# One DMA queue in a listed order, and batch 1's affine pass on ScalarE, in the backward pass of a strided convolution with group norm and GELU

## The chip, the cores and the metric

The kernel runs on 1 core of one Trainium2 chip. The metric is the device time of one execution in microseconds, from the launch's first to its last instruction. The core has a matrix engine (TensorE, PE in the profile; its weight loads are PEld), three engines for elementwise work (VectorE or DVE, ScalarE or ACT, GpSimd or POOL), and SyncE (SP), which here issues transfers only. Each engine runs its own instructions in the order in which they were emitted and waits on semaphores for the others.

## The reference

Forward and backward of a convolution stem: two sequences of 16,000 positions and 256 channels, a kernel of 31 taps with stride 2, a normalisation of each channel over the positions, and GELU.

```python
L = (T - K) // s + 1                       # 7985 positions out, K = 31, s = 2
h = einsum('blc,cd->bld', x[:, 0:s*L:s], w[0])
for i in range(1, K):
    h = h + einsum('blc,cd->bld', x[:, i:i + s*L:s], w[i])
mu  = h.sum(1) / L
var = ((h - mu) ** 2).sum(1) / L
h = (h - mu) / sqrt(var + 1e-5) * gn_gamma + gn_beta
out = gelu(h)                              # tanh form
```

The kernel returns `out` and, for a given `grad_out`, the gradients of `x`, `w`, `gn_gamma` and `gn_beta` (`out_0` to `out_4`). All data is bf16.

## The kernel before, in words

The work runs in five stages, whose names the planner uses. **F0** and **F1** are the forward convolution of batch 0 and batch 1, **G0** and **G1** the gradient of x for the two batches, and **W** is the gradient of w. Each batch's sequence is cut into four chunks of 2,048 output positions. The convolutions are done with fewer multiplications, by a scheme of sums and differences in three nested levels: each level has three branches, called A, B and C, and B uses a sum of the two others' inputs. VectorE forms the sums (`f_sums` L472, `g_sums` L985, `w_add` L1251, `pair_x`, `pair_d` and the subtractions L1413), TensorE multiplies (`f_mm` L508, `g_mm` L1033, `w_mm` L1289), and VectorE combines the branches in PSUM (`ve` L583 and `ve_neg` L587, called by `f_seed` and `g_seed`). ScalarE moves finished banks out of PSUM (`keep` L591, `f_evac` L611 and L624, and the copies L540, L573, L1060, L1070, L1370). PSUM has four slots of two banks, `ring`, which are taken in turn.

- *x.* `x_load` (L399) brings a chunk of x transposed into the one buffer `XT` by `turn` (L344), a transposing transfer on SP: one transfer of 2.2 MB for a chunk, but four of a quarter's size for the very first.
- *h.* The forward stores h in the DRAM tiles `hd` and its sums for the statistics (`fwd_stats`).
- *GELU.* `gelu_batch` (L790) goes through a batch in 16 units (`gelu_unit` L829). A unit loads h (L833, on ACT's own queue), works with five ScalarE instructions (L836, L838, L842, L844, L860) and some ten of VectorE (L840, L846, L850, L862), stores the gradient of h's normalised form in `dyd`, and the output in out_0 (batch 0, turned on SP) or in `yd` (batch 1, turned later by `out0_late`). Batch 0's units run beside F1, batch 1's beside G0.
- *Gradient with respect to h.* `e_load` (L928) brings a chunk of `dyd` and `hd` (1 MB each), `e_comp` (L932) forms dy*a + h*b + c by two affine passes (L938, L941) and an addition (L943), and `spread` (L950) copies the result into `ET`, the layout that TensorE reads: four copies a chunk, on ACT for batch 0 (L953) and on VectorE for batch 1 (L955), by `COPY`. `dn_turn` (L977) turns the same chunk and stores it in `dnd`.
- *Second differences.* `d2_piece` (L1180) loads a piece of `dnd`, forms differences of it (L1196) and stores them in `d2d` by five transfers; there are seven pieces for a batch, with one buffer `DT` for the piece and one or two for the differences. W reads `d2d` in two loads a step (`d_tile`) and x in 1 MB loads (`x_raw`). Seven pieces of batch 0 and seven of batch 1 run beside G1.

The order of all this is not the order of the calls. `Plan.add` (L151) records each instruction with an estimated duration and the bytes that it reads and writes. `Plan.order` (L180) gives each a due time, counted back from the instructions that need its result, and then walks through the instructions as a list scheduler: at each step the engine that is free first takes, of the instructions whose inputs are ready, the one that is due first. `slack`, `look` (how many TensorE groups it may take out of turn), `pads` (how much of its spare time a transfer is held back) and `lead`, a table of shifts for kinds of instructions by stage, name and caller, set the order. `emit` (L258) gives out the instructions in the order that was found, so that each engine's queue has exactly this order. The planner's picture of the transfers is one server that takes them one after another (`server`, L237 to L240), with eight places for SP and eight for POOL.

Transfers go through three queues: plain loads and all turns through SP (hardware descriptors, q1 in the profile), stores through POOL (L341 with "POOL"; software descriptors, q0), and the loads of h in `gelu_unit` through ACT (q10). `PACE` spreads the GELU units' due times over their stage. `GO` (L1117) names the branches of the input gradient in which a second group of products is split by `g_outer`.

Of the kernel before, what the change touches and what calls it, by code (L numbers as in the profile page):

```python
# [13 lines left out]
ALU = mybir.AluOpType  # L14
# [24 lines left out]
class Plan:  # L39
# [3 lines left out]
    def __init__(self, tc):  # L43
        self.tc = tc
        self.ops = []
        self.lastw = {}
        self.readers = {}
        self.pe = 0.0
        self.slack = 120.0
        self.hold = -1  # L50
        self.look = 11
        self.pads = (270.0, 253.5, 0.0)
        self.lead = {
            "F0 f_mm f_leaf": 4.0,
            "F0 f_mm f_outer": -1.5,
            "F0 f_mm f_three_ac": 5.5,
            "F0 f_mm pe_turn": 7.5,
            "F0 f_three_b forward": -7.5,
            "F0 keep f_evac": -4.0,
            "F0 load f_evac": 10.5,  # L60
            "F0 load load_w": -2.5,
            "F0 load put": 2.0,
            "F0 tt f_sums": 7.5,
            "F0 tt third": -5.0,
            "F0 turn w2_part": -1.5,
            "F0 turn x_load": -5.0,
            "F0 ve f_seed": -2.0,
            "F0 w_sub f_first": 7.5,
            "F1 f_evac last": -7.5,
            "F1 f_mm f_leaf": -5.0,  # L70
            "F1 f_mm f_three_ac": 1.5,
            "F1 gelu_unit gelu_batch": -3.0,
            "F1 load gelu_unit": 2.5,
            "F1 tiny fwd_stats": -4.0,
            "F1 tt gelu_unit": 1.0,
            "F1 turn gelu_batch": -6.5,
            "F1 turn x_load": -5.0,
            "F1 ve f_seed": 6.5,
            "F1 zero gelu_batch": 11.0,
            "G0 e_comp conv_stem_kernel": -3.0,  # L80
            "G0 g_mm g_leaf": -11.0,
            "G0 g_mm g_three_ac": 5.0,
            "G0 g_mm g_three_b": -4.0,
            "G0 gelu_unit gelu_batch": -0.5,
            "G0 keep g_evac": -3.5,
            "G0 load dgb_store": 7.0,
            "G0 load dn_turn": -8.0,
            "G0 load e_load": 4.5,
            "G0 load g_evac": -8.0,
            "G0 load gelu_unit": 10.0,  # L90
            "G0 load load_w2": 5.0,
            "G0 tiny elem_finalize": 1.5,
            "G0 tt first": 5.0,
            "G0 tt second": 6.0,
            "G0 tt third": 5.5,
            "G0 turn dgb_store": -3.0,
            "G0 turn dn_turn": 1.0,
            "G0 turn gelu_batch": -8.5,
            "G0 ve g_seed": 3.5,
            "G0 ve_neg g_seed": 8.0,  # L100
            "G1 e_comp conv_stem_kernel": -10.0,
            "G1 g_mm g_outer": 3.5,
            "G1 g_mm g_three_ac": 0.5,
            "G1 g_mm g_three_b": 0.5,
            "G1 g_three_b input_grad": 2.5,
            "G1 keep g_evac": -3.5,
            "G1 load dn_turn": 0.5,
            "G1 load e_load": -4.0,
            "G1 load g_evac": 5.5,
            "G1 spread e_comp": -9.5,  # L110
            "G1 tt first": 10.5,
            "G1 tt second": -4.5,
            "G1 tt third": -5.0,
            "G1 zero e_comp": -5.0,
            "W keep weight_grad": 4.0,
            "W load d_tile": -15.5,
            "W load w_emit": -8.5,
            "W ve w_done": 5.0,
            "W ve weight_grad": 9.0,
            "W w_add weight_grad": 2.5,  # L120
            "W w_emit w_done": 7.5,
            "W w_mm w_pairs": -1.5,
            "W w_mm w_single": -1.0,
        }
        self.overlap = {"DVE": 0.084, "ACT": 0.1}
        self.npe = 0
        self.stage = "F0"
# [23 lines left out]
    def add(self, eng, dur, outs, ins, fn, dma=None, slack=None):  # L151
# [24 lines left out]
        self.ops.append(dict(eng=eng, kind=kind, dur=dur, fn=fn, preds=preds, dma=dma, at=self.pe, hold=-1 if eng == "PE" else self.hold,  # L176
# [3 lines left out]
    def order(self):  # L180
# [7 lines left out]
        for i in range(n - 1, -1, -1):  # L188
            o = ops[i]
            full = o["dur"] + (1.3 * o["dma"] + 6.0 if o["dma"] is not None else 0.15)  # L190
            end = o["at"] if o["eng"] == "PE" else o["at"] + o["slack"]
            for s in succ[i]:
                end = min(end, due[s])
            due[i] = end - full - self.lead.get(o["kind"], 0.0)
        left = [len(o["preds"]) for o in ops]
        ready = [0.0] * n
        wait = {e: [] for e in ("PE", "DVE", "ACT", "POOL", "SP")}
        pes = [i for i, o in enumerate(ops) if o["eng"] == "PE"]
        rank = {i: k for k, i in enumerate(pes)}
        nextpe = 0  # L200
        gone = set()
        lanes = [[0.0] * 8, [0.0] * 8]
        for i in range(n):
            if not left[i]:
                wait[ops[i]["eng"]].append(i)
        free = {e: 0.0 for e in wait}
        server = 0.0
        start = [0.0] * n
        ends = [0.0] * n
        done = 0  # L210
        while done < n:
            best = None
            for e, w in wait.items():
                if e == "PE":
                    w = [i for i in w if rank[i] < nextpe + self.look]
                else:
                    w = [i for i in w if ops[i]["hold"] <= nextpe]
                if w:
                    t = max(free[e], min(ready[i] for i in w))
                    if best is None or t < best[0]:  # L220
                        best = (t, e, w)
            t, e, w = best
            i = min((i for i in w if ready[i] <= t + 1e-9), key=lambda i: (due[i], i))
            wait[e].remove(i)
            o = ops[i]
            if o["dma"] is not None:
                lane = lanes[e == "POOL"]
                t = max(t, lane.pop(0))
            start[i] = t
            end = t + o["dur"]  # L230
            free[e] = end - self.overlap.get(e, 0.0)
# [5 lines left out]
            if o["dma"] is not None:  # L237
                server = max(server, end + 1.3) + o["dma"]
                end = server + 0.9
                lane.append(end)  # L240
            ends[i] = end
            done += 1
            slip = free["PE"] - due[pes[nextpe]] - ops[pes[nextpe]]["dur"] if nextpe < len(pes) else 0.0
            for s in succ[i]:
                r = end + 0.034 * (e != "PE") if ops[s]["eng"] == e and o["dma"] is None else end + 0.12
                room = max(0.0, due[s] + slip - r)
                if ops[s]["dma"] is not None:
                    r += min(self.pads[0 if o["dma"] is None else 1], 0.3 * room)
                elif o["dma"] is not None and ops[s]["eng"] != "PE":
                    r += min(self.pads[2], 0.3 * room)  # L250
                ready[s] = max(ready[s], r)
                left[s] -= 1
                if not left[s]:
                    wait[ops[s]["eng"]].append(s)
        self.start, self.ends = start, ends
        return sorted(range(n), key=lambda i: (start[i], i))
# [13 lines left out]
def conv_stem_kernel(  # L270
# [64 lines left out]
    def dcost(nbytes, run):  # L335
        ns = {256: 18, 512: 27, 1024: 46, 2048: 85, 4096: 165}[run]
        return nbytes / run * ns / 16e3 * 1.1

    def load(out, in_, nbytes, run, eng="SP", slack=None, issue=None):
        e = {"SP": nc.sync, "POOL": nc.gpsimd, "ACT": nc.scalar}[eng]  # L340
        add(eng, issue or {"POOL": 0.8, "SP": 0.4, "ACT": 0.15}[eng], [out], [in_], lambda: e.dma_start(out=out, in_=in_),  # L341
            dma=dcost(nbytes, run), slack=slack)

    def turn(out, in_, nbytes, slack=None):  # L344
        add("SP", 1.25 + max(0, nbytes - 262144) * 6e-6, [out], [in_],
            lambda: nc.sync.dma_start_transpose(out=out, in_=in_), dma=dcost(nbytes, 256), slack=slack)
# [52 lines left out]
    def x_load(b, c):  # L399
# [4 lines left out]
        if b == 0 and c == 0:  # L404
            rows = [sb(REG + 4096 * g, 4, 512) for g in range(3)]
            for g, nm in enumerate((P, P, 16)):
                load(rows[g][0:nm], src[P * g:P * g + nm].rearrange("m (j o f) -> m j o f", j=4, o=2)[:, :, 1, :], nm * 4096, 1024)
# [5 lines left out]
        else:  # L413
            turn(flat[:, :, 0:nr], src, nr * 8192)
# [28 lines left out]
    def load_w(sl):  # L443
# [3 lines left out]
        for ch in range(2):  # L447
            for br, r1 in ((A, 0), (C_, 1)):
                i0 = 4 * r2 + 2 * r1
                for par in range(2):  # L450
# [3 lines left out]
                         65536 * nq, 512, issue=0.8)  # L454
# [471 lines left out]
    COPY = ("ACT", "DVE")  # L926
# [5 lines left out]
    def e_comp(b, c):  # L932
        et = ET[(4 * b + c) % 2]
        for dh in range(2):
            hv, ev = (t[:, dh].rearrange("p e k f -> p (e k f)") for t in (EH, EG))
            s4, s5, s6 = st(b, 4, dh), st(b, 5, dh), st(b, 6, dh)
            add("DVE", dve(2048, 4), [hv], [hv, s5, s6],
                lambda hv=hv, s5=s5, s6=s6: nc.vector.tensor_scalar(out=hv, in0=hv, scalar1=s5, scalar2=s6,  # L938
                                                                    op0=ALU.mult, op1=ALU.add))
            add("DVE", dve(2048, 4), [ev], [ev, s4],  # L940
                lambda ev=ev, s4=s4: nc.vector.tensor_scalar(out=ev, in0=ev, scalar1=s4, scalar2=None, op0=ALU.mult))  # L941
# [175 lines left out]
    GO = {(1, br) for br in (B_, C_, A, )}  # L1117
# [361 lines left out]
    PACE = ((5.0, 19.0), (391.0, 67.0))  # L1479
# [91 lines left out]
```

## Time and profile before

| what | value |
|---|---|
| time, median of 3 runs | 1235.54 us (1235.24 to 1240.54) |
| profiled execution | 1234.47 us, its span 1232.3 us |
| mean granted clock of TensorE | 0.992 |
| matmuls (PE), count and busy time | 7,846, 1195.2 us |
| DVE / ACT / POOL busy | 1010.3 / 535.8 / 203.7 us |
| moved by DMA | 263.56 MB, 214 GB/s on average |
| stages F0, F1, G0, G1, W begin at about | 0, 215, 447, 677, 890 us |
| SP transfers landing: turns of x, median | 13.6 us |
| SP transfers landing: 1 MB of x in W, median | 9.6 us |
| ACT's loads of h (256 KB), median to landing | 4.6 us |

The page has one row for each engine with its busy time. A slice row shows forty equal parts of the span, each with a digit for the busy tenths. A chain of waits follows the work that ended last back in time: 31% of the span are matmuls of the forward (L508), 27% of the weight gradient (L1289), 21% of the input gradient (L1033), and no other line has more than 2%. Two more lines from the list of waits (engine, its line, what it waited for, then the total, the number of times and the longest):

```profile
SPq L346 <- DVE arena L476: 116.6, 10, 41.8
SPq L341 <- PE ps L1289: 114.9, 25, 21.6
...
POOL out_dram L341 <- DVE arena L1321: 292.0, 14, 158.8
POOL d2d L341 <- DVE arena L1196: 110.7, 48, 8.4
```

SP and POOL spend much of their time waiting for the data of the next transfer or for its buffer.

### The profile page before, as it was taken

The numbers are of one execution on the slowest core, as the hardware profiler recorded it, in microseconds if no ns is written. First come the engines' busy times: TensorE is split into PE (matmuls) and PEld (weight loads), VectorE is DVE, ScalarE is ACT, GpSimd is POOL, SyncE is SP. The second block draws the span as 40 slices with busy tenths as digits, with TensorE's granted clock in tenths as the row PEclk, the third lists the DMA queues.
The fourth block names the chain that finished last, engine by engine and source line by source line (L and its number), as shares of the span: only waits on it lengthen the run. The fifth ranks groups of instructions, "written<-read, shape, count | busy, mean of one in ns | idle before, by whom it ended". The sixth has DMA issues, their size and how long they took to land.

```text
span 1232.3 us, 19408 instructions
## 1 busy us (share of the span) xinstructions
PE 1195.2 (97%) x7846; PEld 768.7 (62%) x7846; DVE 1010.3 (82%) x1297; ACT 535.8 (43%) x769; POOL 203.7 (17%) x321
## 2 busy tenths in 40 slices
PE   6999999899999999999999999999999999999998
PEld 4888899577676964444444444444466554566865
DVE  7988798597979859989887889888776986778883
ACT  1243344565768468888783334444322111012200
POOL 1020231011111203211210323333210000011031
PEclk8999999899999999999999999999999999999999
DMA  9642979866695896686636888886899499986562
GB/s 205 108 111 63 191 198 177 168 139 158 127 201 159 258 317 208 231 248 168 213 120 182 254 273 313 245 308 251 300 305 326 145 318 319 320 293 218 179 170 69
DMA packets 283545, 263.56 MB, mean 214 GB/s; under 512 B 186815, under 2 KB 254446, under 8 KB 275184
## 3 DMA queue, kind: packets, MB, share of 16 engines
q1 hardware_dynamic: 255808, 166.38, 52.5%
q0 software_dynamic: 23040, 87.55, 20.1%
q10 hardware_dynamic: 4608, 8.39, 2.3%
q8 instruction: 61, 1.00, 0.3%
q14 instruction: 28, 0.23, 0.1%
HBM read 129.44 MB, written 87.52 MB: 176 GB/s over the span
## 4 chain that ended last, share of the span: by engine, by line
PE 79%; DVE 6%; DMA 6%; issue 4%; ACT 2%; POOL 2%; SPq 0%; POOLq 0%; ACTq 0%; DVEq 0%
PE ps L508 31%; PE ps L1289 27%; PE ps L1033 21%; DMA d2d<-arena 2%; DMA arena<-hd 1%; DVE arena L1196 1%; POOL d2d L341 1%; DVE arena L476 1%; DMA out_dram<-arena 1%; DVE ps L583 1%; DMA arena<-in_x_dram 1%; DVE arena L466 1%; DMA arena<-arena 1%; DMA arena<-in_w_dram 1%; DVE arena L943 0%
## 5 line engine op out<-in xcount | busy, mean ns | idle before, releaser
L1033 PE MATMUL ps<-arena 128*128 128x512 bf16 (+1 forms) x2016 | 435.9, 378 | 11.8 <-DVE ps L583 8.3
L508 PE MATMUL ps<-arena 128*128 128x256 bf16 (+4 forms) x3552 | 426.7, 282 | 12.6 <-DMA arena<-in_x_dram 6.9
L508 PEld LDWEIGHTS <-arena 128*128 128x128 bf16 x3552 | 347.8, 99 | 94.4 <-issue 13.7
L1033 PEld LDWEIGHTS <-arena 128*128 128x128 bf16 x2016 | 198.0, 98 | 249.4 <-issue 20.1
L1289 PE MATMUL ps<-arena 128*128 128x256 bf16 (+1 forms) x2176 | 332.5, 313 | 0.0
L1289 PEld LDWEIGHTS <-arena 128*128 128x128 bf16 x2176 | 212.8, 98 | 112.6
L591 ACT ACTIVATE arena<-ps 128x1024 f32<-128x1024 f32 (+1 forms) x143 | 146.1, 1022 | 277.8 <-PE ps L1033 79.9
L476 DVE TENSOR_TENSOR arena<-arena 128x1087 bf16<-128x1087 bf16 (+3 forms) x194 | 163.7, 889 | 27.5 <-PE ps L508 27.2
L850 DVE TENSOR_TENSOR arena<-arena 128x1024 bf16<-128x1024 bf16 x160 | 109.0, 689 | 14.8 <-ACT arena L842 8.2
L1252 DVE TENSOR_TENSOR arena<-arena 128x4096 bf16<-128x4096 bf16 x42 | 95.8, 2288 | 25.2 <-PE ps L1289 19.6
L583 DVE TENSOR_TENSOR ps<-ps,arena 128x1024 f32<-128x1024 f32 x77 | 94.0, 1229 | 27.0 <-PE ps L1289 13.3
L341 POOL DMA_DIRECT2D out_dram<-arena x75 | 54.1, 741 | 365.7 <-DVE arena L1321 292.0
L992 DVE TENSOR_TENSOR arena<-arena 128x516 bf16<-128x516 bf16 (+3 forms) x176 | 83.5, 513 | 16.4 <-PE ps L1033 10.0
L1196 DVE TENSOR_TENSOR arena<-arena 128x768 bf16<-128x768 bf16 (+3 forms) x112 | 65.5, 642 | 16.7 <-DMA d2d<-arena 15.6
L341 POOL DMA_DIRECT2D d2d<-arena x70 | 51.0, 729 | 112.3 <-DVE arena L1196 110.7
L611 ACT ACTIVATE arena<-ps 128x512 bf16<-128x512 f32 (+1 forms) x64 | 36.8, 578 | 74.5 <-PE ps L508 74.5
L840 DVE SCALAR_TENSOR_TENSOR arena<-arena 128x1024 bf16<-128x1024 bf16 x32 | 39.2, 1224 | 20.1 <-ACT arena L838 19.8
L583 DVE TENSOR_TENSOR ps<-arena,ps 128x1024 f32<-128x1024 f32 x43 | 52.8, 1227 | 3.2 <-PE ps L1033 2.7
L1370 ACT COPY ps<-ps 128x512 f32<-128x512 f32 x28 | 16.0, 571 | 87.6 <-PE ps L1289 87.6
L1060 ACT ACTIVATE ps<-ps 128x512 f32<-128x512 f32 x48 | 27.9, 582 | 58.8 <-PE ps L1033 58.6
L1413 DVE TENSOR_TENSOR arena<-arena 128x2304 bf16<-128x2304 bf16 x36 | 48.0, 1354 | 5.5 <-PE ps L1289 5.5
L341 POOL DMA_DIRECT2D dyd<-arena x32 | 17.6, 550 | 194.2 <-DVE arena L850 189.5
(87 smaller groups left out, 785.8 us busy)
## 6 DMA issues: line engine op xcount, KB each, us to landing
arena<-in_x_dram SPq DMA_DIRECT2D x52, 1024.0 KB, 9.6
arena<-d2d SPq DMA_DIRECT2D x16, 1216.0 KB, 11.9
out_dram<-arena POOLq DMA_DIRECT2D x14, 1024.0 KB, 5.9
d2d<-arena POOLq DMA_DIRECT2D x30, 384.0 KB, 6.3
arena<-dnd SPq DMA_DIRECT2D x10, 960.0 KB, 6.4
vl<-arena POOLq DMA_DIRECT2D x36, 256.0 KB, 4.8
arena<-vl SPq DMA_DIRECT2D x9, 1024.0 KB, 8.6
hd<-arena POOLq DMA_DIRECT2D x8, 1024.0 KB, 6.3
```

What stands on the lines that cost most here:

```text
L341: add(eng, issue or {"POOL": 0.8, "SP": 0.4, "ACT": 0.15}[eng], [out], [in_], lambda: e.dma_start(out=out, in_=in_), dma=dcost(nbytes, run ...
L476: lambda: nc.vector.tensor_tensor(out=o, in0=a, in1=b, op=ALU.add))
L508: yield nc.tensor.matmul(ps[:, dh, cs], lhsT=wt, rhs=mv, start=s0, stop=False, skip_group_check=True)
L583: add("DVE", dve(1024, 1), [out], [a, b], lambda: nc.vector.tensor_tensor(out=out, in0=a, in1=b, op=op))
L591: lambda: nc.scalar.activation(out=out, in_=ps, func=ACT.Copy, scale=scale))
L850: add("DVE", dve(1024), [o], [a, b_], lambda: V.tensor_tensor(out=o, in0=a, in1=b_, op=op))
L992: lambda: nc.vector.tensor_tensor(out=o, in0=a, in1=b, op=ALU.add))
L1033: yield nc.tensor.matmul(ps[:, e, 0:wide], lhsT=lt, rhs=mv, start=s0, stop=False, skip_group_check=True)
L1196: lambda: nc.vector.tensor_tensor(out=out, in0=a, in1=b_, op=ALU.subtract))
L1252: add("DVE", dve(4096), [o], [a, b], lambda: nc.vector.tensor_tensor(out=o, in0=a, in1=b, op=ALU.add))
L1289: yield nc.tensor.matmul(ps[:, s, c0:c1], lhsT=lt, rhs=mv, start=s0, stop=False, skip_group_check=True)
L1413: add("DVE", dve(2304), [DL[i3, b]], [D2[b]], lambda b=b, i3=i3, o_=o_: nc.vector.tensor_tensor(out=DL[i3, b], in0=D2[b][:, o_:o_ + 17:2, ...
```

## The change

All transfers of more than 4,096 bytes go to SP, whatever the call says. Turns of x are cut into four for every chunk. For batch 1, `e_comp`'s two affine passes are ScalarE instructions, and `COPY` puts its spread on ScalarE as well. The walk of the planner becomes a function of its own, `listing`, with a finer picture of the transfers: only the first transfer of each queue moves at a time, two queues in the air share the engines by weights (`SH`), small packets in one of two queues multiply the cost (`mixed`), SP stands still when more than `room` packets are under way, and each size of packet has a duration (`PK`). All parameters of the order (`slack`, `look`, `pads`, `lead`, `PACE`) have new values. `GO` is written in another way; its members are (1, B), (1, C) and (1, A) in both versions.

```diff
-        self.slack = 120.0
+        self.slack = 20.0
-        self.look = 11
-        self.pads = (270.0, 253.5, 0.0)
+        self.look = 14
+        self.pads = (582.0, 557.0, 161.0)
         self.lead = {
...
+        self.room, self.mixed = 2048.0, 2.2
...
+        def flow(t):
+            nonlocal now
+            if total > 0:
+                for x in air:
+                    if x["act"]:
+                        x["rem"] -= (t - now) * x["tp"] / total
+            now = t
+        def inflight():
+            return sum(x["rem"] * 16e3 / ops[x["i"]]["ns"] for x in air if ops[x["i"]]["eng"] == "SP")
...
+            heads = {}
+            for x in air:
+                x["act"] = heads.setdefault(ops[x["i"]]["eng"], x) is x and x["on"]
+            total = sum(x["tp"] for x in air if x["act"])
+            if total > max((x["tp"] for x in air if x["act"]), default=0.0) and any(ops[x["i"]]["ns"] < 20.0 for x in air if x["act"]):
+                total *= self.mixed
...
+    ONE = ("F0", "F1", "G0", "G1", "W")
+    SH = {256: 36.0, 512: 56.0, 1024: 70.0, 2048: 100.0, 4096: 168.0, 8192: 310.0}
+    PK = {256: 18.0, 512: 28.0, 1024: 46.0, 2048: 84.0, 4096: 168.0, 8192: 310.0}
+    def load(out, in_, nbytes, run, eng="SP", slack=None):
+        if plan.stage in ONE and nbytes > 4096:
+            eng = "SP"
         e = {"SP": nc.sync, "POOL": nc.gpsimd, "ACT": nc.scalar}[eng]
...
         else:
-            turn(flat[:, :, 0:nr], src, nr * 8192)
+            for j in range(4):
+                turn(flat[:, 8 * j:8 * j + 8, 0:nr], src[:, 1024 * j:1024 * j + 1024], nr * 2048)
...
-    COPY = ("ACT", "DVE")
+    COPY = ("ACT", "ACT")
...
+            if b == 0:
+                add("DVE", dve(2048, 4), [hv], [hv, s5, s6], ...)
+                add("DVE", dve(2048, 4), [ev], [ev, s4], ...)
+            else:
+                add("ACT", act(2048, 0.18), [hv], [hv, s5, s6],
+                    lambda hv=hv, s5=s5, s6=s6: nc.scalar.activation(out=hv, in_=hv, func=ACT.Identity, bias=s6, scale=s5))
+                add("ACT", act(2048, 0.18), [ev], [ev, s4],
+                    lambda ev=ev, s4=s4: nc.scalar.activation(out=ev, in_=ev, func=ACT.Identity, scale=s4))
...
-    GO = {(1, br) for br in (B_, C_, A, )}
+    GO = {(1, br) for br in ORDER}
...
-    PACE = ((5.0, 19.0), (391.0, 67.0))
+    PACE = ((109.0, 7.0), (327.0, 2.5))
```

274 lines of the change are left out of this document (154 added, 120 removed).

## The prediction

> **What bounds the kernel now.** I read the busy table and the slices first, then a table by stage, then the waits, then the timeline around each gap of TensorE.
>
> ```profile
> span 1232.3 us, 19408 instructions
> PE 1195.2 (97%) x7846; PEld 768.7 (62%) x7846; DVE 1010.3 (82%) x1297; ACT 535.8 (43%) x769; POOL 203.7 (17%) x321
> PEclk8999999899999999999999999999999999999999
> ...
> q1 hardware_dynamic: 255808, 166.38, 52.5%
> q0 software_dynamic: 23040, 87.55, 20.1%
> ```
>
> TensorE (PE) is busy for 97% and idle for 37.1 us in all, so whatever moves, the gain is bounded by that. The stages (us, PE, PEld, DVE, ACT, POOL, clock, DMA share, GB/s):
>
> ```profile
> 0.00:21.50 21.50, 10.56 (x72) 7.05 (x72) 13.02 (x21) 3.21 (x3) 3.28 (x11) 0.84 0.94 244
> 21.50:215.00 193.50, 193.47 (x1754) 171.51 (x1755) 170.07 (x196) 74.45 (x162) 30.25 (x44) 1.00 0.72 140
> 215.00:447.00 232.00, 222.37 (x1771) 173.45 (x1769) 188.75 (x283) 143.61 (x218) 28.76 (x48) 0.99 0.75 179
> 447.00:677.00 230.00, 226.45 (x1059) 103.81 (x1057) 194.81 (x310) 173.11 (x203) 43.34 (x74) 0.99 0.67 206
> 677.00:890.00 213.00, 204.72 (x951) 92.74 (x949) 185.70 (x282) 86.00 (x118) 67.55 (x103) 1.00 0.84 277
> 890.00:1228.00 338.00, 337.63 (x2248) 220.10 (x2247) 257.61 (x209) 55.40 (x67) 29.84 (x40) 0.99 0.77 246
> ```
>
> Batch 0's forward (second row) and the weight gradient (last row) have no gap: the change can only lose there. Idle time sits in the start (10.9 us), batch 1's forward beside the first GELU (9.6), batch 0's input gradient (3.6), batch 1's (8.3) and the tail (4.7). The largest gap, in the timeline (start, duration, what, then the idle time before it and who ended it):
>
> ```profile
> 216.92 20.43 SPq L346 DMA_TRANSPOSE arena<-in_x_dram  x1
> ...
> 219.53 0.91 ACTq L341 DMA_DIRECT2D arena<-hd  x2
> ...
> 232.73 1.24 ACT L836 ACTIVATE arena<-arena,stats 128x1024 bf16<-128x1024 bf16 x1 [10.14 <-DMA arena<-hd]
> ...
> 241.42 0.37 PE L508 MATMUL ps<-zt 128*128 128x256 bf16 x1 [6.11 <-ACT arena L591]
> ```
>
> A 2.2 MB turn of x runs for 20 us on SP; the h loads issued on ACT's queue beside it need 13.1 and 15.5 us (2.4 at best elsewhere); ACT is in order, so `keep` (L591), which empties the bank that TensorE needs, stands behind two GELU units and TensorE waits 6.11 us. The second gap is the end of batch 1's input gradient:
>
> ```profile
> 886.44 2.29 DVE L1252 TENSOR_TENSOR arena<-arena 128x4096 bf16<-128x4096 bf16 x1 [1.13 <-DMA arena<-in_x_dram]
> 888.65 1.23 DVE L583 TENSOR_TENSOR ps<-ps,arena 128x1024 f32<-128x1024 f32 x1
> 889.92 5.30 PE L1033 MATMUL ps<-arena 128*128 128x512 bf16 x16 [2.40 <-DVE ps L583]
> ```
>
> The last seed (L583) stands on VectorE behind an addition for the next stage, which waits for a load of x. The 16 matmuls after it take 5.30 us, where 16 at the usual spacing (L1033: 435.9 us for 2016, 0.216 each) take 3.46: the granted clock was 0.5 for 3.4 us there. It was so after the gaps of 6.11 (6.8 us), 2.12 (3.4) and 2.40 us (3.4), so these cost another 3.4, 1.7 and 1.7 us.
>
> The Trainium skill, page "TensorE: Matmul & The Clock Gate", section "HAM oscillation — how this bites in real kernels", gives as the rule no idle gaps over some 3.4 us; by it the two short gaps would cost no clock and the step at the end of the input gradient would be worth 2.4 us instead of 4.1. The trace speaks against it for these two gaps, and for it at 716.8 us, where a gap of 2.08 us left the clock alone.
>
> **The change, part by part.** Times are set against the profiled execution's own 1234.5 us (span 1232.3 and 2.2 around it); the runs' median is 1235.5, so the forecast serves both.
>
> 1. *First GELU units.* In the changed order ACT's first `keep` stands ahead of all GELU work and the second behind two instructions of one unit (2 x 1.23 us) instead of behind two units and a table load. The h loads go to SP, the first behind one quarter of a turn: 11.8 us for a turn alone (the one issued at 39.9), so 3 us for a quarter; from 217 that is some 220, plus 2.4 to land: just when the statistics are done (223.2). The gap of 6.11 and its 3.4 us at half clock go; I book 1 us for what is left: **-8.5** (0 to -9.5; nothing if the load waits for the quarters behind it too).
> 2. *End of the input gradient.* In the new order on VectorE the last seed stands ahead of the addition that waits for x. Worth up to 2.40 + 1.7 = 4.1.
> 3. *Batch 1's affine pass and spread to ACT.* VectorE loses 8 x 0.812 (L938), 8 x 0.750 (L941), 8 x 0.559 and 8 x 0.298 us (L955): 19.4 of its 185.7 in a stage of 213. ACT has no row for an affine pass of 2048: 1.231 us for 1024 (L836, scale and bias by pointer) and 0.83 ns for each further element (L953: 1.464 at 1536, 0.614 at 512) make 2.08; 16 of them and the spread (8 x 1.464 + 8 x 0.614) add 49.9 us to ACT's 86.0. That is hidden: in batch 0's input gradient ACT was busy for 173 of 230 us, with the same copies, and TensorE lost 3.6. A chunk's chain of load, affine, spread grows by some 6 us, covered by the 53 us between chunks; uncovered, it would cost 4 x 6. The small gaps that seeds late on VectorE leave in this stage (2.08, 0.46, 0.32, 0.54, 0.40, 0.35, 1.34) add to 5.5; half of it, 2.7.
> 4. *What is late next.* Items 2 and 3 pull the weight gradient's start forward by 6.8 us, but it also needs the second differences (`d2_piece`): 14 pieces one after another, load, subtractions, five stores, from 674.0 to 878.1 us (14.6 each), then both D2 loads, landed at 889.4 and 892.4. The stage's first matmul ran at 895.1: a margin of 2.7. So of the 6.8 I book **-3.5**, 2.7 and a little for subtractions that start earlier on a freer VectorE. Bounds 0 and -9.6.
> 5. *One queue.* SP issues 208 transfers now; 253 come from POOL, 32 from ACT, and 7 turns become 28: 514. At the median issue times of 0.32 (long rows) to 1.5 us (turns), the 306 more are 100 to 460 us; SP waits some 990 us in its own list of waits, which hides them. Small pieces cost more by hardware descriptors: 512 bytes took 27 ns and 1024 took 46, POOL's 4096 took 165. For about 26 MB in 512-byte and 9.4 MB in 1024-byte pieces this adds 23 us to 925 us of DMA time, 75% to 77% of the span. SP alone reached 0.96 in 924.0 to 954.8 us with POOL at rest, so one queue can carry it. What is new is order: a store that waits for its data holds every load behind it. Cover: the loads are issued ahead of use, and a turn of x no longer shares engines with POOL's stores (11.8 us alone, 19.8 to 22.5 beside them). I book **+1** (0 to +37, the second rival).
> 6. *Nothing.* The set `GO` has the same three members before and after, so the two "more" leaves do not exist: TensorE has 15,694 rows in both orders. "ACT" and "POOL" in calls of `load` are overruled above 4096 bytes. The other gaps (2.12 and 1.7 at 448.5, 1.92, 1.60, 0.80, 0.64: 8.8) come from ACT's order, rewritten throughout; I book 0, bounds -8.8 and +9.5 (another gap like the largest). Start and tail keep their chains: 0, within 2.
>
> The Trainium skill, page "DMA: Bandwidth & Descriptors", section "Issuing engines are not separate DMA queues", says that issuing from several engines saves only the time to start the transfers. By it, merging can gain nothing and adds issue time; the h loads' 15.5 us against 2.4 speak against taking it for latency. By it alone item 1 would rest on ACT's order only, half of it, and the sum would be 1228.
>
> Sum: -8.5 - 3.5 + 1 = -11: **1223 us**, 1.0% faster.
>
> **The rivals.**
> *All gaps close* (10%): items 1 to 3 in full and the 8.8: -9.5 - 9.6 - 8.8 = -27.9, 1207. For it: every order was rewritten, and ACT's share before 677 is lower without its 32 issues. Against: the margin of 2.7 us in item 4.
> *The second differences become the bound* (22%, slower). A piece's loads and stores now stand in line behind 1 MB transfers (out_1, dyd, hd, x) and behind stores that wait. VectorE waited 15.6 us for such stores in eight waits already, and a store issued at 704.1 needed 11.0 us to land. One 1 MB row is 3.5 us of the queue; 3 us more for each of batch 1's seven pieces is 21, less the margin 2.7 is 18; over all 14 pieces 39. With item 1 kept: 1234.5 - 8.5 + 18 + 1.7 = 1246, and up to 1267. It decides from 1.2 us a piece, where it eats item 1. Against: the number of difference stores ahead of each out_1 store is within 3 of what it was.
> *x comes late in the forward* (11%, slower). The tile of x has one buffer; its fourth quarter can stand behind a GELU store whose data is late. SP's waits for such data average 6.4 us (51.5 in 8, L862); three chunks by 6.4 and 1.7 of half clock each are 24, less 11: 1247. For: the quarters are issued between loads and stores of GELU units. Against: a chunk has 58 us and a turn needs 12.
> *Nothing net* (12%): the h load waits as before, the new queue's small waits eat the rest: 1234, within 0.5%.
>
> **How the numbers follow.** 45% for the forecast (its own range 1215 to 1229), 10, 22, 11 and 12 for the others. The measurement can tell about 0.5%, 6 us. Faster by more: 45 + 10 = 55%; within it: 12%; slower: 33%. The range goes down to 1208, where the first rival begins, and up to 1252, which takes in the lower half of the second and the third: some 18% stay outside.
>
> **What would show it.** Right: no wait of `keep` behind an h load near 235 us and no half clock there; DVE near 166 and ACT near 136 us in batch 1's input gradient, ACT's affine pass near 2.08 us; the gap before the last seed gone, and the weight gradient's first matmul released by D2 or VectorE. Wrong: VectorE waiting for d2d stores for more than 15.6 us, TensorE idle before its first L1289 (now without a gap), gaps before L508 with a turn of x as releaser, or gaps in the weight gradient, which has none.

## The result, and the profile after

| | median | range, runs | ratio to before, same chip (95% interval) |
|---|---|---|---|
| before | 1235.39 us | 1233.85 to 1240.54, 4 | |
| changed | 1218.97 us | 1218.41 to 1219.35, 4 | 0.9853 [0.9814, 0.9893] |

The change makes the kernel 1.5% faster. The profiled execution took 1218.80 us (before: 1234.47), its span is 15.3 us shorter. Two later runs of a slower state, one of the kernel before (1249.76 us) and one of the kernel with two moves (1251.41), are left out of the figures below. The busy table, the granted clock by slice and the largest queue:

```profile
span 1217.0 us, 19291 instructions
PE 1186.9 (98%) x7782; PEld 767.1 (63%) x7846; DVE 992.4 (82%) x1265; ACT 580.7 (48%) x801; POOL 23.0 (2%) x68
...
PEclk9999999999999999999999999999999999999999
...
q1 hardware_dynamic: 344586, 262.31, 75.7%
```

GpSimd (POOL) no longer issues these stores, and the granted clock is at 90% or more in every slice (a 9). The clock records of the trace before have four stretches at half clock, 6.8 us from 13.9 and 239.1, 3.4 from 450.8 and 891.1; after the change there is none before the last matmul. In those 20.4 us TensorE was busy for 16.8 (5.56, 4.48, 3.40 and 3.40); half of that, 8.4, is regained clock. Its idle time (span less busy) falls from 37.1 to 30.1 us. Together that is 15.4, the whole difference of the spans. The split is good to a few us only, as 64 matmul records are missing in the profile after (7,782 of 7,846), which can make its idle time look longer. The stages (us, PE, PEld, DVE, ACT, POOL, clock, DMA share, GB/s):

```profile
0.00:21.50 21.50, 9.48 (x67) 6.64 (x68) 11.24 (x20) 3.31 (x3) 3.34 (x11) 1.00 0.92 234
21.50:215.00 193.50, 190.09 (x1711) 166.96 (x1709) 166.65 (x191) 70.87 (x151) 1.86 (x3) 1.00 0.62 135
215.00:445.00 230.00, 226.55 (x1824) 177.84 (x1823) 193.57 (x291) 150.83 (x235) 3.49 (x10) 1.00 0.83 208
445.00:671.00 226.00, 223.63 (x1038) 103.45 (x1058) 189.79 (x302) 181.75 (x204) 8.92 (x24) 1.00 0.63 187
671.00:879.40 208.40, 205.38 (x942) 93.95 (x960) 175.63 (x259) 118.71 (x141) 4.91 (x19) 1.00 0.89 286
879.40:1213.20 333.80, 331.76 (x2211) 218.28 (x2231) 254.82 (x207) 55.28 (x67) 0.53 (x1) 1.00 0.81 247
```

TensorE's idle time by stage, before and after: start 10.9 and 12.0, F0 0.0 and 3.4, F1 9.6 and 3.5, G0 3.6 and 2.4, G1 8.3 and 3.0. So in idle time F1 and G1 gave the gain; F0, which had no gap, now has five, of 0.48 and 0.78 us. The two places that the prediction showed, in the timeline after (start, duration, engine, line; L900 is the first GELU operation, L1322 `w_add`, L1359 the weight gradient's matmul; the bracket is idle time and its releaser):

```profile
223.82 2.44 SPq L408 DMA_TRANSPOSE arena<-in_x_dram  x1
...
231.87 1.02 ACT L655 ACTIVATE arena<-ps 128x1024 f32<-128x1024 f32 x1 [1.66 <-PE ps L572]
235.66 1.24 ACT L900 ACTIVATE arena<-arena,stats 128x1024 bf16<-128x1024 bf16 x1 [1.16 <-issue]
```

```profile
875.44 2.28 DVE L1322 TENSOR_TENSOR arena<-arena 128x4096 bf16<-128x4096 bf16 x1
879.49 0.27 PE L1359 MATMUL ps<-zt 128*128 128x256 bf16 x1
...
880.47 0.60 PE L1359 MATMUL ps<-arena 128*128 128x256 bf16 x4 [0.27 <-DMA arena<-d2d]
```

The first quarter of the turn of x holds SP for 2.44 us (the next two for 3.55 and 5.64), where the whole turn held it for 20.43; `keep` (L655) runs ahead of the first GELU operation, and no gap over 0.3 us stands between 181 and 264 us. The addition no longer has a seed behind it, and TensorE runs through into the weight gradient, where a second difference (`d2d`) is 0.27 us late. All that looks as predicted. The experiments say that the reason is another one.

### The profile page after: what moved, and what is told of

Same layout as the page of the kernel before. It is cut to its first block, busy times and chain, and to the rows that moved or that the text cites. A ratio compares the mean times of both kernels' runs of the same rounds, so it can differ in the third digit from the quotient of the medians.

```text
span 1217.0 us, 19291 instructions
## 1 busy us (share of the span) xinstructions
PE 1186.9 (98%) x7782; PEld 767.1 (63%) x7846; DVE 992.4 (82%) x1265; ACT 580.7 (48%) x801; POOL 23.0 (2%) x68
## 3 DMA queue, kind: packets, MB, share of 16 engines
q1 hardware_dynamic: 344586, 262.31, 75.7%
## 4 chain that ended last, share of the span: by engine, by line
PE 83%; DVE 6%; ACT 4%; DMA 4%; issue 2%; SPq 0%; another core or an unknown queue 0%; POOL 0%; DVEq 0%; ACTq 0%; POOLq 0%
PE ps L572 28%; PE ps L1103 28%; PE ps L1359 26%; DMA arena<-in_x_dram 2%; DVE arena L530 2%; ACT arena L675 1%; DVE arena L540 1%; DVE arena L1266 1%; DMA arena<-dnd 1%; DMA d2d<-arena 1%; DVE arena L914 1%; DVE ps L647 1%; ACT arena L688 1%; ACT arena L1009 1%; DVE arena L647 0%
## 5 line engine op out<-in xcount | busy, mean ns | idle before, releaser
L572 PE MATMUL ps<-arena 128*128 128x256 bf16 (+4 forms) x3552 | 425.3, 281 | 15.4 <-DMA arena<-in_x_dram 9.0
L1103 PE MATMUL ps<-arena 128*128 128x512 bf16 (+1 forms) x1975 | 429.8, 376 | 5.4 <-DVE ps L647 2.1
L1359 PE MATMUL ps<-arena 128*128 128x256 bf16 (+1 forms) x2153 | 331.6, 313 | 2.0 <-DVE arena L1483 0.5
L655 ACT ACTIVATE arena<-ps 128x1024 f32<-128x1024 f32 (+1 forms) x143 | 145.6, 1020 | 302.3 <-PE ps L1359 76.8
L1359 PEld LDWEIGHTS <-arena 128*128 128x128 bf16 x2176 | 212.9, 98 | 113.4 <-issue 1.2
L540 DVE TENSOR_TENSOR arena<-arena 128x1088 bf16<-128x1088 bf16 (+3 forms) x194 | 163.2, 882 | 14.5 <-PE ps L572 14.2
L1322 DVE TENSOR_TENSOR arena<-arena 128x4096 bf16<-128x4096 bf16 x42 | 95.5, 2285 | 25.3 <-PE ps L1359 18.4
L1062 DVE TENSOR_TENSOR arena<-arena 128x516 bf16<-128x516 bf16 (+3 forms) x176 | 82.3, 507 | 10.9 <-PE ps L1103 10.7
L1266 DVE TENSOR_TENSOR arena<-arena 128x768 bf16<-128x768 bf16 (+3 forms) x112 | 65.9, 636 | 10.9 <-DMA d2d<-arena 5.6
L647 DVE TENSOR_TENSOR arena<-arena 128x1024 f32<-128x1024 f32 x32 | 38.8, 1220 | 15.1 <-ACT arena L1140 7.2
L530 DVE TENSOR_TENSOR arena<-arena 128x2048 bf16<-128x2048 bf16 (+1 forms) x45 | 42.3, 979 | 0.7 <-DMA arena<-vl 0.7
L924 ACT ACTIVATE arena<-arena 128x1024 bf16<-128x1024 bf16 x32 | 33.6, 1050 | 15.3 <-DVE arena L914 15.3
L900 ACT ACTIVATE arena<-arena,stats 128x1024 bf16<-128x1024 bf16 x32 | 39.3, 1229 | 2.0 <-issue 1.2
```

What stands on the lines that cost most here:

```text
L530: add("DVE", dve(n), [o], [a, b], lambda: nc.vector.tensor_tensor(out=o, in0=a, in1=b, op=ALU.subtract))
L540: lambda: nc.vector.tensor_tensor(out=o, in0=a, in1=b, op=ALU.add))
L572: yield nc.tensor.matmul(ps[:, dh, cs], lhsT=wt, rhs=mv, start=s0, stop=False, skip_group_check=True)
L647: add("DVE", dve(1024, 1), [out], [a, b], lambda: nc.vector.tensor_tensor(out=out, in0=a, in1=b, op=op))
L655: lambda: nc.scalar.activation(out=out, in_=ps, func=ACT.Copy, scale=scale))
L1062: lambda: nc.vector.tensor_tensor(out=o, in0=a, in1=b, op=ALU.add))
```

## The experiments

The theory on record: the gain is the new order (first GELU units, last seed, affine pass), and the one queue costs about nothing. The rival: it is the one queue. In the captions "old order" is the order of the kernel before, "one queue" means that every transfer over 4,096 bytes is issued by SP.

**The changed order on the three old queues.** Only the issuing engine is put back:

```diff
 def load(out, in_, nbytes, run, eng="SP", slack=None):
+    q = "SP" if plan.stage == "F0" and eng == "ACT" else eng
     if plan.stage in ONE and nbytes > 4096:
         eng = "SP"
-    e = {"SP": nc.sync, "POOL": nc.gpsimd, "ACT": nc.scalar}[eng]
+    e = {"SP": nc.sync, "POOL": nc.gpsimd, "ACT": nc.scalar}[q]
```

> The changed kernel with its order kept instruction for instruction, but its stores issued by POOL and its h loads by ACT again, as before the change. Theory (the order of the engines' instructions is the gain, the one queue by itself is worth nothing): 1216 to 1224 us, no gap near 235 us. Rival (the one queue is the gain, since turns and loads no longer share the engines with POOL's stores): 1230 us or more, with h loads of 10 us or more and the gap before the first keep back.

Measured: 1255.67 us (1250.81 to 1260.62; the run profiled is the longest of its four), ratio 1.016 [1.0101, 1.0218]. The order alone makes the kernel slower; the theory falls. TensorE's two longest waits there (engine, line, what it waited for: total, times, longest):

```profile
PE ps L573 <- ACT ps L605: 10.8, 5, 7.3
PE ps L1104 <- ACT arena L656: 10.6, 2, 10.1
```

L605 is a copy that stands on ScalarE between GELU operations, L656 is `keep`. What ScalarE waited for ahead of them:

```profile
246.98 1.24 ACT L901 ACTIVATE arena<-arena,stats 128x1024 bf16<-128x1024 bf16 x1 [12.64 <-DMA arena<-hd]
...
542.65 1.02 ACT L656 ACTIVATE arena<-ps 128x1024 bf16<-128x1024 f32 x1 [12.50 <-DMA out_dram<-arena]
```

The gap at 246 us is the same kind as before near 235: the first GELU operation waits for a load of h, and the copy stands behind it. At 534 no GELU operation is in the way: `keep` itself waits until a store to `out_dram`, issued by GpSimd, has landed and frees its buffer.

**One queue, old order.** The counterpart: nothing else of the change, no split turns, no affine pass on ScalarE.

```diff
-        e = {"SP": nc.sync, "POOL": nc.gpsimd, "ACT": nc.scalar}[eng]
+        e = nc.sync if nbytes > 4096 else {"SP": nc.sync, "POOL": nc.gpsimd, "ACT": nc.scalar}[eng]
```

> The kernel before with its order kept, but every transfer above 4096 bytes issued by SP. Theory (the queue gives nothing by itself, and in an order that was not listed for it stores that wait hold loads behind them): 1236 to 1265 us, the gap of 6 us near 235 still there, and VectorE or TensorE waiting for loads of x, d2d or dnd. Rival (the one queue is the gain): 1228 us or less.

Measured: 1217.78 us (1216.74 to 1218.28), ratio 0.985 [0.9808, 0.9892]: the whole gain. The new order, the split turns and the affine pass together add nothing that shows (0.9853 for the full change, with nearly the same interval). The turn of x that took 20.43 us of SP takes 11.26 here, and though ScalarE's order is the old one, its first GELU operation starts at 224.6 us instead of 232.7:

```profile
220.83 11.26 SPq L346 DMA_TRANSPOSE arena<-in_x_dram  x1
224.62 1.24 ACT L836 ACTIVATE arena<-arena,stats 128x1024 bf16<-128x1024 bf16 x1 [2.13 <-DMA vl<-arena]
```

The small gaps in G1 are gone too, but for one of 0.25 us and the one before the last seed (3.07), with the affine pass still on VectorE. What VectorE waited for there (L1196, in the changed kernel L1266, are the subtractions of `d2_piece`, 671 to 895 us), in the kernel before, with one queue in the old order, and in the changed kernel:

```profile
DVE arena L1196 <- DMA d2d<-arena: 15.6, 8, 3.5
```

```profile
DVE arena L1196 <- DMA d2d<-arena: 1.0, 2, 0.6
```

```profile
DVE arena L1266 <- DMA d2d<-arena: 5.6, 5, 2.2
```

VectorE was late in G1 because it stood in front of buffers whose stores had not landed. The largest of these gaps in the kernel before, 2.08 us at 716.8, shows it: the subtraction waits, the seed stands behind it, and TensorE waits for the seed.

```profile
715.16 1.03 DVE L1196 TENSOR_TENSOR arena<-arena 128x768 bf16<-128x768 bf16 x2 [3.50 <-DMA d2d<-arena]
...
717.58 1.22 DVE L583 TENSOR_TENSOR ps<-arena,ps 128x1024 f32<-128x1024 f32 x1
```

The one queue takes most of that wait away, so in the old order G1 did not need a VectorE with less work. Why the stores land sooner is open: the median of the 384 KB stores of `d2d` falls from 6.3 to 3.0 us, and no run tells fewer neighbours on the engines from the change of the issuing queue.

**The affine pass alone.** The changed kernel with batch 1's affine passes and spread back on VectorE, at the same places of the order (in `e_comp`, and L1023 of `spread`):

```diff
-                add("ACT", act(2048, 0.18), [hv], [hv, s5, s6],
-                    lambda hv=hv, s5=s5, s6=s6: nc.scalar.activation(out=hv, in_=hv, func=ACT.Identity, bias=s6, scale=s5))
+                    lambda hv=hv, s5=s5, s6=s6: nc.vector.tensor_scalar(out=hv, in0=hv, scalar1=s5, scalar2=s6, ...)
```

> The changed kernel with its order kept, but batch 1's affine pass and spread issued to VectorE (19.4 us there) instead of ScalarE (50 us there). Theory (the relief of VectorE is worth about what was booked, 2 to 4 us, because the second differences set the start of the weight gradient): 1219 to 1224 us, the last d2d store of the stage issued 2 to 6 us later than at 859.7. Rival (the relief carries the whole gain of the input gradient): 1226 to 1230 us, with gaps of 5 us and more in batch 1's input gradient.

Measured: 1224.17 us (1223.05 to 1225.99), ratio 0.9906 [0.987, 0.9942]. In the changed order the move is worth some 5 us by the profiles: without it a gap of 3.19 us opens at 729 us, with 3.4 us of half clock behind it, and the weight gradient starts at 884.8 instead of 879.5. The ratios say it less sharply, as their intervals overlap a little. VectorE is busy for 188.0 us of G1 instead of 175.6. In the old order with one queue the same work on VectorE leaves one gap of 0.25 us in G1 ahead of the last seed, so there is next to nothing for the move to gain; no run made it there. It pays for a place that the new order has made tight.

**The two order moves on the kernel before.** `keep` ahead of the first GELU unit, and the last seed ahead of the addition, with the old queues (shortened, comments added):

```diff
+        w.remove(k)                      # ACT: first keep of F1
+        w.insert(w.index(g), k)          # ahead of its first GELU operation
+        w.remove(s)                      # DVE: last seed
+        w.insert(w.index(a), s)          # ahead of w_add
```

> The kernel before with two instructions moved: ACT's first keep of batch 1's forward ahead of the first GELU unit, and the last seed of the input gradient ahead of the second addition of the weight gradient on VectorE. Theory (order): the first gap falls from 6.11 to below 1.5 us and its 6.8 us at half clock go, 8 to 9 us; the second gives at most the 2.7 us by which the second differences were early: 1223 to 1228 us. Rival (the late h loads, so the queues, cause the first gap): the gap only moves to the next ACT instruction that TensorE needs, and the time stays at 1232 to 1236.

Measured: 1247.40 us (1232.69 to 1250.71, 9 runs), ratio 1.007 [1.003, 1.0109], slower than both numbers on record. The first gap only moved (5.06 us at 238, with 3.4 us of half clock), because the load of h was still late. And a new one opened in the weight gradient, the longest of the kernel. The wait on TensorE, and what SP did 20 us earlier:

```profile
PE ps L1332 <- DMA arena<-d2d: 9.1, 1, 9.1
```

```profile
887.53 30.90 SPq L389 DMA_TRANSPOSE arena<-yd  x2
```

Two turns of `yd` held SP for 30.9 us (17.6 in the profile before) beside one store of out_1 on GpSimd's queue, whose 104 packets ran from 895 to 916 us (from 901 to 904 before), and the load of the second differences behind them started at 919.9. So the collision is not tied to one place: a changed order can meet it elsewhere.

**Which transfers.** Three kernels in the old order: only ScalarE's loads of h on SP; only GpSimd's stores on SP; one queue only for the stages G1 and W (the same line in each, shortened):

```diff
+        e = nc.sync if eng == "ACT" else {...}[eng]                            # loads of h
+        e = nc.sync if eng == "POOL" and nbytes > 4096 else {...}[eng]         # stores
+        e = nc.sync if nbytes > 4096 and plan.stage in ("G1", "W") else {...}[eng]   # late stages
```

> Before's order; the 4096-byte-run loads of h that ScalarE issued go through SP's queue, all stores stay on GpSimd's. If what the one queue saves is ScalarE being held at its h-load issues, most of the gain of the run with one queue and the old order (1235 to 1218) should be here: 1218 to 1225. If it is GpSimd's stores running beside SP's turns and loads, the gap near 235 stays or gets longer and the time is 1230 to 1245.

> Before's order; GpSimd's stores go through SP's queue, the h loads stay on ScalarE's. If GpSimd's stores beside SP's turns are the cost, this alone gives 1217 to 1222, with no gap over 1 us near 235 and none of the gaps at 717 to 830. If ScalarE's h loads are the cost, 1228 to 1240 with the gap near 235 of 5 to 7 us left.

> Before's order; one queue only for the work planned from batch 1's input gradient on (the rest keeps its three queues). If the gain is spread over the kernel, the gap near 235 (6.1 us and 3.4 us of half clock regained) stays and the time is 1226 to 1232. If all of it is collisions of stores with the turns and loads of the second half and of the weight gradient, 1217 to 1222. If it is the first half alone, 1233 to 1238.

Measured, beside a before of 1234.4:

| on SP | median | range, runs | ratio |
|---|---|---|---|
| loads of h | 1228.48 | 1226.41 to 1232.87, 10 | 0.9953 [0.9934, 0.9972] |
| stores | 1219.52 | 1218.32 to 1220.24, 4 | 0.9873 [0.9838, 0.9909] |
| all, G1 and W only | 1228.33 | 1221.24 to 1231.82, 10 | 0.9948 [0.9923, 0.9973] |

The stores are the gain. The loads of h alone bring a third of it, between the two numbers on record: the gap near 235 us goes, but one stays in F1, 3.47 us at 261, because the turn of x beside them now takes 29.6 us of SP. With one queue in the late stages only, the gap at 240 (5.54 us) and its 6.8 us of half clock are back and the gaps of G1 are gone: the gain comes from both halves.

**Does any second queue do it?** One queue in the old order, but the eight 1 MB stores of h (8,192-byte packets) go out by ScalarE, or by GpSimd:

```diff
-                load(h_d[b][c][:], hs..., 1 << 20, 4096, "POOL", slack=60.0)
+                load(h_d[b][c][:], hs..., 1 << 20, 4096, "POOL", slack=60.0, at=nc.scalar)   # or nc.gpsimd
```

> The run with one queue in the old order (1217.8), but its eight 1 MB stores of h are issued by ScalarE, so they travel on a second hardware queue beside SP's. If bytes of any second queue hold up SP's turns, the 1 MB turns of x that have such a store beside them take 4 to 8 us longer on SP than in the run with one queue (7.6 to 11.3 us) and the time rises to 1219 to 1226. If only GpSimd's software queue does it, the turns stay at 8 to 11 us and the time at 1217 to 1219.

> As the run before it, but GpSimd issues the eight stores of h. If any second queue holds up SP's turns, this gives the same as the run with ScalarE's queue, within 2 us, and the turns of x beside a store take 4 to 8 us longer. If the software queue alone does it, 1219 to 1226 here and 1217 to 1219 there. If the stores of h do not matter and the small stores do, 1217 to 1219 in both.

(The turns of x named in these texts as of 1 MB are of 2.2 MB.) Measured: 1220.28 us (1215.27 to 1226.41, 6 runs, ratio 0.9863 [0.9833, 0.9892]) on ScalarE's queue and 1218.67 (1216.95 to 1221.51, 4 runs, 0.9857 [0.983, 0.9885]) on GpSimd's; with one queue it was 1217.78. The medians do not tell the three apart. The profile does, for one run, since the run profiled with ScalarE's queue is the longest of its six (1226.41). SP's timeline, VectorE's, and the table of two stretches of 10 us, there:

```profile
222.05 30.14 SPq L347 DMA_TRANSPOSE arena<-in_x_dram  x1
```

```profile
255.15 7.44 DVE L477 TENSOR_TENSOR arena<-arena 128x1088 bf16<-128x1088 bf16 x8 [6.91 <-DMA arena<-in_x_dram]
```

```profile
232.00:242.00 10.00, 10.00 (x78) 7.36 (x77) 9.29 (x15) 8.09 (x10) 0.00 (x0) 1.00 1.20 86
242.00:252.00 10.00, 10.00 (x78) 7.37 (x76) 6.23 (x7) 2.42 (x6) 0.00 (x0) 1.00 1.26 111
```

And ten us of the same turn with one queue in the old order, where it ran from 220.8 to 232.1:

```profile
222.00:232.00 10.00, 10.00 (x77) 7.18 (x75) 5.28 (x13) 7.65 (x8) 0.00 (x0) 1.00 1.14 248
```

The last two columns are the lesson. The DMA share adds up the times for which packets are open, so it can exceed 1. In both kernels it is as high (1.20 and 1.14), but beside the other queue the engines move 86 GB/s and without it 248. Of the turn's own 256-byte packets 1,388 start in those ten us, against 7,045. The store gets slower as well, VectorE waits 6.91 us for x, and a gap of 4.46 us opens on TensorE at 261, with 6.8 us of half clock. In the trace's packets from 230 to 245 us of the span, a 256-byte packet of the turn is open for 91 to 162 ns on average over 3 us; without company it is 18. The three whole turns ahead of this one took 13.4, 11.1 and 12.5 us of SP, against 9.1, 7.6 and 10.5 with one queue. Counted over whole profiles, by what another queue started in the same microsecond (packets of 256 bytes started in 1 us, and in how many microseconds that happened):

```
                                  no other   512 to 4,096 B   8,192 B
before                            640 (173)   388 (141)       241 (48)
loads of h on SP                  644 (171)   384 (135)       243 (62)
h stores on ScalarE's queue       597 (279)      -            224 (47)
h stores on GpSimd's queue        595 (289)      -            282 (18)
one queue, old order              605 (287)      -            413 (8)
```

So a turn is held up by a hardware queue (ScalarE's, 224) and by the software queue (GpSimd's, 241) alike. On GpSimd's queue the stores of h met a turn in 18 microseconds only, and the turns of x took their usual 7.7 to 10.5 us: that run is no test of the software queue, the run with the loads of h alone is. The Trainium skill, page "DMA: Bandwidth & Descriptors", section "Queues, rings and completion order", says that each engine goes round the queues that have work, a packet at a time. The counts agree in that both queues advance side by side; how the turns are shared out they do not show, since 1,388 packets of 256 bytes and 62 of 8,192 started from 232 to 242 us. It is the rule that I should have set beside the 13 and 15 us of the loads of h.

**Three tries for a better version.** The changed kernel with ScalarE's evacuations ahead of the squares (its part of the statistics of h); one queue in the old order with many moves (evacuations and last seeds on ScalarE ahead of squares and of up to four GELU operations, last seed on VectorE ahead of the addition); and the same without passing GELU operations:

```diff
+            if a.get("tag") == "square" and b.get("tag") == "evac" and w[k + 1] not in self.ops[w[k]]["preds"]:
+                w[k], w[k + 1] = w[k + 1], w[k]
```

> The changed kernel with each evacuation of the second half of a unit moved on ScalarE ahead of the square of the first half, which it stood behind in the changed order. The page of the changed kernel has TensorE gaps of 0.48 and 0.78 us at 67, 115, 131, 164 and 180 us that end on this evacuation: 3.3 us together. If they are on the path, 1214 to 1217; if TensorE's wait is paid elsewhere (the square then ends late and its sums are waited for at the end of the batch), 1218 to 1221.

> One queue in the old order (1217.8; TensorE gaps of 1.92, 1.60, 2.11 and 3.07 us at 308, 380, 440 and 872 us, the last two with 3.4 us of half clock each, which costs half of that), and on ScalarE each evacuation and last seed ahead of the squares and up to four GELU operations before it, on VectorE the last seed ahead of the addition that waits for x. If these waits are set by the order of the instructions alone: 2.1 + 3.1 + 3.4 less, and some of 3.5, 1208 to 1212. If the gaps move to the next wait, as when the same kind of move was made with three queues: 1215 to 1220.

> One queue in the old order, with only these moves: on ScalarE evacuations and last seeds pass the squares ahead of them (no GELU operation is passed, unlike the run with all moves), and on VectorE the last seed passes the addition that waits for x. The gap of 2.11 us at 440 waits for two squares of 1.15 us and should go with its half clock (1.7), the one of 3.07 at 872 should shrink to the 2.1 that the run with all moves had there (a load of second differences): about 1213, range 1211 to 1216. If the loss of the run with all moves came from the squares and not from the GELU operations: 1220 to 1230.

Measured: 1216.71 us (1216.01 to 1217.19), ratio 0.9851 [0.9816, 0.9886] for the first; 1230.82 (1229.09 to 1235.0), 0.9964 [0.9947, 0.9982]; and 1221.75 (1220.08 to 1226.64), 0.9896 [0.9861, 0.9932]. In the first the three gaps of 0.78 us in F0 are gone and the span is 1.8 us shorter than the changed kernel's, as expected; its ratio can't be told from 0.9853, so it is a candidate and not a proven gain. The second missed its numbers; the third missed its 1213 and fell into the range on record for a loss that comes from passing the squares. In the last one the gap of 2.11 at 440 shrank to 0.94 and the one of 3.07 at 872 to 0.8, but a new one stands behind `keep` (L636) in the first row:

```profile
PE ps L1079 <- ACT ps L636: 4.4, 1, 4.4
...
PE ps L1335 <- DMA arena<-d2d: 0.8, 1, 0.8
```

Moves by hand cost more than the gaps they closed; which of them opened the 4.4 us was not tried. These two kernels also spread over some 6 us from run to run with one queue (8 runs each), against 1.5 for the old order (4 runs), and that too is open.

## Why the prediction was right, and where it was not

The time (1223 predicted, 1218.97 measured) fell into the range, on the side forecast. That was in good part luck: 8.5 us were booked for the first GELU units, whose new order gives nothing on the old queues, and the one queue, which by itself gives the whole gain, was booked as a small cost.

- *Step 5, one queue: booked +1, measured -15 to -20.* This is the step that failed. One queue in the old order is 1217.78 against 1237.45 for the kernel before on the same chip, and stores alone 1219.52 against 1234.4. The prediction had the rows for it: turns of 11.8 us alone and 19.8 to 22.5 beside stores, loads of h of 13 and 15.5 us instead of 2.4. It named the turns as cover for the cost of the queue and gave them no price of their own. The new planner has such a price: `mixed`, 2.2, by which small packets beside another queue cost more. The feared cost, stores that wait for data in front of loads, did not show: the DMA share of SP's queue is 75.7% (77 estimated), and VectorE's wait for stores of `d2d` fell from 15.6 to 5.6 us, though the stores' own times are mixed (median 4.8 us instead of 6.3 for 384 KB, 5.6 instead of 3.9 for 192 KB).
- *Step 1, first GELU units: booked -8.5.* The gap and its half clock went, but not through ScalarE's order. With the order alone the gap moved (5.06 us at 238); with the queue alone it vanished in the old order. The step's other half, loads of h on SP, was nearer: alone it removed this gap, left one of 3.47 at 261 and was worth some 6 us in all. `keep` behind the GELU units was what one saw; the late load was the cause. The 3.4 us for half clock were too many: TensorE was busy for 4.48 of those 6.8 us, so 2.2.
- *Step 2, the last seed: up to 4.1.* Right for its own gap: 2.40 us in the kernel before, 3.07 with one queue in the old order, none after. It does not add up: in the last try the seed moved and the time did not follow.
- *Step 3, affine pass.* ScalarE's affine pass takes 2.08 us, as estimated from shorter rows. VectorE has 175.6 us in G1 (166 forecast) and ScalarE 118.7 (136), since some of the passes, from 642.5 us on, run in G0 already. Booked 2.7, it is worth some 5 in the changed order; in the old one with one queue little was left for it to gain (not tried).
- *Step 4, second differences: margin 2.7, cap -3.5.* They now hold up the weight gradient's first matmuls by 0.27 us, so this reading held. With the gap of 0.50 at 891 it is also the sign of being wrong that the prediction named, gaps in the weight gradient, if a small one. The cap was too tight: the last store of a piece is issued at 859.7 us instead of 875.6, as VectorE no longer waits for 10 of its 15.6 us.
- *Step 6, nothing.* The leaves of `GO` are the same, start and tail stayed within 2 us. The gap at 448.5 and its half clock went (-3.8), and F0 got 3.4 us of gaps that were not foreseen.

Of the rivals, the second differences as a slower bound had the mechanism the wrong way round: in one line VectorE waits less for their stores. x was not late in the forward. The rival that all gaps close came near in G1 and F1, but not in F0 and at the start.

On the clock, the rule of gaps over some 3.4 us (the Trainium skill, page "TensorE: Matmul & The Clock Gate", section "HAM oscillation — how this bites in real kernels") fits no better than in the trace before. The gap of 2.12 us at the start of G0 was followed by 3.4 us at half clock with only the stores on SP, and by none with only the loads of h on SP, where a gap of 3.47 us at 261 left the clock alone as well.

## What to carry to other kernels

When transfers in 256-byte packets (transposing ones here) share the DMA engines with another queue's large packets, look at GB/s beside the DMA share. Here engines with the same share moved a third of the bytes when queues were in each other's way, and putting the stores into the same queue, behind the turn, was worth more than any order of the instructions that was tried. An instruction that stands behind a waiting one is not yet the cause; ask what the waiting one waits for, and price the row that shows a transfer at twice its time alone. Before a gain is given to one part of a change, run that part alone: here one line made all of it, and moves made to close the gaps one sees opened others.

## What was not expected of the hardware

- Two queues can cut what the DMA engines move to a third: 86 GB/s at a share of 1.20 against 248 at 1.14, both while a turn of x runs.
- A turn holds SP until its packets are nearly through (30.1 of 33.1 us to landing), so a slowed turn also stops every issue behind it: 30.9 us for two turns of `yd`, with the next stage's loads behind.
- The spread from run to run goes with it in part: the kernel before ranged from 1226.2 to 1246.9 us over all its runs, the old order with one queue from 1216.7 to 1218.3, and with only the stores of h on ScalarE's queue from 1215.3 to 1226.4. That collisions that happen in some runs only are the reason is likely for the last, whose longest run was profiled; for the kernel before it was not shown, as there is one profile of it.
